# Making the next slice's token operands from set 3 on, with another sum and high-part tile, and one buffer each for the gated rows and P1's copy

## The chip, the cores and the metric

The kernel runs on one core of a Trainium2 chip. The metric is the time of the whole program on the device, in microseconds (us). Of the core's engines five matter here: TensorE (PE; matrix products, with the weight loads shown as PEld), VectorE (DVE), ScalarE (ACT), GpSimd (POOL) and SyncE (SP), of which the last two mostly issue DMAs in this program. TensorE writes its results into PSUM, 8 banks of 128 x 512 numbers; the operands lie in SBUF; large intermediates go to DRAM and come back by DMA.

## What is computed

A linear attention is followed by two layers, both of them chains of matrix products, on 3072 tokens. The first layer has a product of two gates, the second a Gelu (the sigmoid form). The change is in the second layer's first product, `x @ w_in`, with the Gelu behind it:

```
for t in range(S):
    state = gamma[None, :, None, None] * state + np.einsum('bhd,bhe->bhde', k[:, :, t], v[:, :, t])
    y[:, :, t] = scale * np.einsum('bhd,bhde->bhe', q[:, :, t], state)
...
a = x @ w1
b = x @ w2
h = a * b @ w3
return (h @ w_out).astype(np.float32)
...
h = x @ w_in                                # 3072 x 512 by 512 x 2048
g = h * (1.0 / (1.0 + np.exp(-1.702 * h)))
return (g @ w_out).astype(np.float32)       # 3072 x 2048 by 2048 x 512
```

All is float32. A product keeps that precision by three matmuls: each operand is split into a high part (`fp32r`) and a low part, what is left of it, and high x high, high x low and low x high are added up in one bank (`mm3`, L256 to L259).

## The kernel before

The program runs in stages: attention with the first gates, the gates (`psm`), the first layer's second half (`blend`, tiles `h`, `wh`), then `Expand` (`x @ w_in` and the Gelu), then `contract` (`g @ w_out`). The change is in `Expand`, in `operands`, which makes its token operands, and in a table of the last stage's opening work.

`Expand` uses a scheme of seven products P1 to P7 in place of eight (Strassen's, in Winograd's form): two blocks of 512 tokens and two halves of the 512 dimensions on one side, a 2 x 2 grid of weight blocks on the other. **A slice** is a pair of token blocks; there are three. **A set** is one call of `quad` (L643): all seven products for one group of 256 of the 2048 columns. A slice has eight sets, numbered 0 to 7 here, so there are 24. One product is 6 matmuls (two 128-row steps, three matmuls each), one set 42.

In a set TensorE makes P1 (bank `a`), P5 (bank `e`), then P4 of the set before (into that set's bank `a`), P6 (added onto P1), P2 (bank `c`), P7 (added onto the same `a`), P3 (added onto P5). ScalarE copies the sums out between them, `s1` after P1, `s5` after P5, `u2` after P6, `u3` after P7 (`copy`, L607), so P6 can't start ahead of the end of the copy `s1`, nor P7 ahead of `u2`. VectorE adds P2 to `s1` (L659), `s5` to `u3` (L662) and P3 to `u2` (L665). The Gelus of a set run in the next set (`fourth`, L619): `g[:, 0]` from `s1`, `b12` from `u2`, then P4, `g[:, 2]` from `u3` and `g[:, 1]` from the bank. The three gated rows in `g` are stored to DRAM (L628), VectorE makes four sums of them into `t` (L636), and `t` is stored too (L637). `s1` and `g` have two buffers, taken in turn (`s0`/`s1`, `g0`/`g1`); `t` has one.

**The token operands** of a slice are seven pairs of high and low tiles, 128 x 1024 each: four quarters of the token blocks (P1: b11, P2: b21, P3: b22, P7 or the like: their sums). `operands` (L516) is a generator that is advanced one step at a time: loads, then sums (`sub`, VectorE), then splits: a cast to the high tile (ScalarE in slices 1 and 2, VectorE for slice 0) and a subtraction on VectorE for the low one. `quad` calls `step(0)` to `step(3)` at four places of a set, behind P4 (0), P6 with the Gelus and sums of the set before (1), P7 (2) and P3 (3). A pair (set, step) in the table `NEXT` advances the next slice's generator there; the loads are at (2, 3), and some steps are left to the first set of the slice that reads the operands (L691). For slice 0 the generator is advanced in the turns of `blend` (`ahead`). The tiles' homes are handed on from product to product by `Homes`: an operand takes the home of one that the old slice has read for the last time.

**The weights** are split likewise by `split_left` in ScalarE and VectorE, seven times in the first sets (`SPLIT`); in slice 0 sets 0 to 5 do one each, in slices 1 and 2 one set each. `OPENING` lists what the last slice does ahead of `contract`: loads of its first operands, splits of them in eight pieces (`opening_split`, VectorE), and the split of its first weight in two halves (`split_w`, L744 and L745, on VectorE).

Each engine runs its instructions in the order in which the code issues them. Stores and loads above are issued on SP's queue; the contraction's first weight is loaded from POOL's.

Of the kernel before, what the change touches and what calls it, by code (L numbers as in the profile page):

```python
# [7 lines left out]
F32 = mybir.dt.float32  # L8
# [37 lines left out]
def tile_kernel(  # L46
# [469 lines left out]
    def operands(s, copy, pool):  # L516
# [26 lines left out]
        yield  # L543
        t, t7 = (pool.tile([P, 2, TB], F32, tag=f"yt{n}", name="yt") for n in range(2))
        sub(t, b12, b11)
        yield
        sub(t7, b22, b12)
        yield
        split("P1", b11, raws[0])
        yield  # L550
        give("P1", "P5")
        split("P5", t, ys_homes.tile("l"))
        sub(t, b22, t)
        yield
        split("P6", t, ys_homes.tile("l"))
        sub(t, b21, t)
        give("P6")
        yield
        give("P2", "P7", "P3", "P4")
        split("P2", b21, raws[3])  # L560
        split("P7", t7, raws[1])
        yield
        split("P3", b22, raws[2])
        yield
        split("P4", t, ys_homes.tile("l"))
        yield
# [26 lines left out]
    class Expand:  # L593
# [25 lines left out]
        def fourth(self):  # L619
            a, s, j, n, s1, u2, u3 = self.open  # L620
            g, b12 = self.value(f"g{n % 2}", 3), self.value("b")
            self.gated(g[:, 0], s1)
            self.gated(b12, u2)
            self.product(a, "P4", s, j)
# [18 lines left out]
        def quad(self, s, j, n, step):  # L643
            a, e, c = (self.bank(x) for x in "aec")
            self.product(a, "P1", s, j, True)
            s1 = self.copy(a, f"s{n % 2}")
            self.product(e, "P5", s, j, True)
            s5 = self.copy(e, "s5")
            fourth = self.fourth() if self.open else iter((0, 0))
            next(fourth)  # L650
# [18 lines left out]
        def run(self):  # L669
# [3 lines left out]
            for n in range(1, NQ - 1):  # L673
                fetch_left(n, nc.sync)
            for tag in ("s1", "s5", "u2", "u3", "s0", "b"):
                self.value(tag)
            for tag, m in (("t", 4), ("g0", 3), ("g1", 3)):
                self.value(tag, m)
            ys_homes.add(self.p, l=3, h=1)
            split_left(1, nc.vector.tensor_copy)  # L680
            for s, order in enumerate(QUADS):
                for at_j, j in enumerate(order):

                    def step(at):
                        nonlocal nxt
                        at = at_j, at
                        more = s + 1 < NS
                        if more and at == (2, 3):
                            nxt = operands(s + 1, nc.scalar.copy, self.py)
                            next(nxt)  # L690
                        elif (more and at in NEXT) or (s and at in ((0, 0), (0, 1), (0, 2))):  # L691
                            next(nxt)
                        if not more:
                            for run in OPENING.get(at, ()):
                                run()

                    self.quad(s, j, s * NQ + at_j, step)
# [5 lines left out]
    SPLIT = {j: j + 2 for j in range(NQ - 2)} | {NQ + 4: 0, 2 * NQ + 2: 7}  # L703
    NEXT = (4, 3), (5, 3), (6, 0), (7, 0), (7, 1)
    RIGHT = dict(P1=0, P2=1, P3=2, P5=3, P6=4, P7=5, P4=6)
# [58 lines left out]
    for n in range(2):  # L764
        OPENING[7, 1 + 2 * n] = [
            lambda n=n: split_w("P1", 5, n * KH, n * KH + KH, nc.vector.tensor_copy)
        ]
    for k, at in enumerate(
        ((4, 1), (4, 2), (4, 3), (5, 0), (5, 1), (5, 3), (6, 1), (6, 3))
    ):  # L770
# [184 lines left out]
    with tc.manual_schedule():  # L955
# [180 lines left out]
        def ahead(n):  # L1136
# [7 lines left out]
            elif early is None:  # L1144
# [3 lines left out]
                )  # L1148
                ys_homes.add(py, l=8, h=7)
                early = operands(0, nc.vector.tensor_copy, py)  # L1150
# [127 lines left out]
```

## Time and profile before

| | us |
|---|---|
| median of three runs | 979.91 |
| the runs | 979.59, 979.91, 981.85 |
| the profiled execution, whole | 981.67 |
| its span, first to last instruction | 979.8 |
| TensorE busy in it | 950.6 (97%) |
| VectorE, ScalarE, GpSimd busy | 706.9 (72%), 430.7 (44%), 227.7 (23%) |
| `Expand`, from its first P1 to the contraction's first matmul | 505.0 to 745.6 |

How to read the rows below. Times are from the start of the span. A row of the timeline gives start and length in us, the engine, the line, the operation, what it writes and reads, the shape and, in brackets, how long the engine stood idle before it and what released it. In the list of waits a row gives who waited for whom, the total in us, how often and the longest. A row of the groups by line gives the busy time in us and the mean length in ns, then idle time before it. A row of the DMA issues gives the number, the size and the us from issue to landing. A row of the windows gives the stretch, each engine's busy time, the granted clock of TensorE as a share of 2.4 GHz, the share of DMA time and GB/s. Names leave out buffer numbers, so `s` is `s0`, `s1` or `s5`, and `g` is `g0` or `g1`.

### The profile page before, as it was taken

The page shows a single profiled execution, that of the slowest core. Times are in us where ns is not written, and L with a number is a line of the kernel's source. Part 1 is how long each engine was busy: PE and PEld are TensorE (multiplying, and loading weights), DVE is VectorE, ACT ScalarE, POOL GpSimd, SP SyncE. Part 2 cuts the span into 40 slices and gives each one's busy share as a digit, 9 for nine tenths or more (in the row PEclk, how much of TensorE's full clock was granted, in tenths as well). Part 3 has the DMA queues.
Part 4 walks back from the last instruction along what each step waited for, and adds up shares of the span by engine and source line. Part 5 has one row for each costly group of instructions (what it writes and reads, how often), then busy time and mean ns, then how long its engine had stood idle before and what let it go on. Part 6 is the DMA issues. An engine that isn't in the chain of part 4 may idle for free.

```text
span 979.8 us, 14573 instructions
## 1 busy us (share of the span) xinstructions
PE 950.6 (97%) x5656; PEld 782.1 (80%) x5656; DVE 706.9 (72%) x857; ACT 430.7 (44%) x643; POOL 227.7 (23%) x281
## 2 busy tenths in 40 slices
PE   5899999999999999999999999998999999999998
PEld 5777877888888888888888877886887888888886
DVE  6898878989889876856975766566577575467652
ACT  4555444432322212744536665554544544354430
POOL 6422000479677884511020000000000000000000
PEclk9999999999999999999999999999999999999999
DMA  9999765679998999899786634843986967766861
GB/s 351 400 351 347 277 205 198 210 248 351 323 369 294 349 344 400 283 344 316 245 304 227 271 156 191 308 177 127 327 306 249 343 236 270 249 213 235 288 228 54
DMA packets 87188, 268.50 MB, mean 274 GB/s; under 512 B 7152, under 2 KB 15600, under 8 KB 79056
## 3 DMA queue, kind: packets, MB, share of 16 engines
q1 hardware_dynamic: 71136, 188.60, 53.9%
q0 software_dynamic: 15840, 78.91, 21.1%
q8 instruction: 44, 0.72, 0.3%
q14 instruction: 24, 0.20, 0.1%
q10 hardware_dynamic: 144, 0.07, 0.0%
HBM read 166.37 MB, written 101.19 MB: 273 GB/s over the span
## 4 chain that ended last, share of the span: by engine, by line
PE 86%; DVE 6%; DMA 4%; ACT 2%; issue 1%; POOL 0%; DVEq 0%; POOLq 0%; ACTq 0%; SPq 0%
PE m L259 12%; PE m L258 12%; PE m L257 12%; PE psm L257 7%; PE psm L258 7%; PE psm L259 7%; PE a L257 4%; PE a L258 4%; PE a L259 4%; DMA qkv<-in_qkv_dram 2%; PE e L258 2%; PE e L259 2%; PE e L257 2%; PE psg L257 2%; PE y L440 1%; DMA raw<-in_w_dram 1%
## 5 line engine op out<-in xcount | busy, mean ns | idle before, releaser
L257 PE MATMUL psm<-xh,wh 128*128 128x512 f32 x320 | 124.5, 389 | 0.0
L258 PE MATMUL psm<-xl,wh 128*128 128x512 f32 x320 | 124.5, 389 | 0.0
L259 PE MATMUL psm<-xh,wl 128*128 128x512 f32 x320 | 124.5, 389 | 0.0
L257 PE MATMUL m<-h,op 128*128 128x512 f32 x320 | 124.5, 389 | 0.0
L259 PE MATMUL m<-h,op 128*128 128x512 f32 x320 | 124.5, 389 | 0.0
L258 PE MATMUL m<-l,op 128*128 128x512 f32 x304 | 118.3, 389 | 0.0
L732 ACT CAST h<-l 128x2048 fp32r<-128x2048 f32 x38 | 72.3, 1914 | 82.5 <-PE m L259 63.6
L733 DVE TENSOR_TENSOR l<-l,h 128x2048 fp32r<-128x2048 f32 x38 | 85.4, 2286 | 17.0 <-ACT h L732 16.9
L738 POOL DMA_DIRECT2D op<-sw x6 | 3.2, 532 | 401.9 <-PE a L259 223.1
L139 ACT ACTIVATE x<-raw 128x512 f32<-128x512 f32 x72 | 46.8, 674 | 71.1 <-DMA raw<-in_wo_dram 38.1
L257 PE MATMUL a<-yh,op 128*128 128x512 f32 x192 | 75.2, 392 | 0.0
L258 PE MATMUL a<-yl,op 128*128 128x512 f32 x192 | 75.0, 391 | 0.0
L259 PE MATMUL a<-yh,op 128*128 128x512 f32 x192 | 74.9, 390 | 0.0
L257 PEld LDWEIGHTS m<-h,op 128*128 128x128 f32 x320 | 60.1, 188 | 12.6
L259 PEld LDWEIGHTS psm<-xh,wl 128*128 128x128 f32 x320 | 60.1, 188 | 12.6
L257 PEld LDWEIGHTS psm<-xh,wh 128*128 128x128 f32 x320 | 60.1, 188 | 12.5
L259 PEld LDWEIGHTS m<-h,op 128*128 128x128 f32 x320 | 60.1, 188 | 12.5
L258 PEld LDWEIGHTS psm<-xl,wh 128*128 128x128 f32 x320 | 60.1, 188 | 12.3
L258 PEld LDWEIGHTS m<-l,op 128*128 128x128 f32 x304 | 57.1, 188 | 11.8
L257 PE MATMUL m<-h,wh 128*128 128x512 f32 x168 | 65.4, 389 | 0.0
L259 PE MATMUL m<-h,wl 128*128 128x512 f32 x168 | 65.4, 389 | 0.0
L173 DVE TENSOR_TENSOR l<-l,h 128x2048 fp32r<-128x2048 f32 x19 | 43.5, 2291 | 21.7 <-ACT h L272 20.2
(172 smaller groups left out, 2102.0 us busy)
## 6 DMA issues: line engine op xcount, KB each, us to landing
l<-gd SPq DMA_DIRECT2D x38, 1024.0 KB, 6.4
gd<-t SPq DMA_DIRECT2D x24, 1024.0 KB, 4.9
qkv<-in_qkv_dram POOLq DMA_DIRECT2D x20, 1024.0 KB, 8.8
l<-hd SPq DMA_DIRECT2D x19, 1024.0 KB, 8.0
gd<-g SPq DMA_DIRECT2D x24, 768.0 KB, 3.3
raw<-in_w_dram SPq DMA_DIRECT2D x30, 512.0 KB, 5.6
hd<-g POOLq DMA_DIRECT2D x12, 1280.0 KB, 7.4
raw<-in_wo_dram SPq DMA_DIRECT2D x24, 512.0 KB, 6.9
```

What stands on the lines that cost most here:

```text
L139: nc.scalar.activation(x, high, AF.Abs, scale=2.0**16)
L173: nc.vector.tensor_tensor(lo, x, hi.bitcast(F32), ALU.subtract)
L257: nc.tensor.matmul(ps, wh, xh, start=start, stop=False, skip_group_check=True)
L258: nc.tensor.matmul(ps, wh, xl, start=False, stop=False, skip_group_check=True)
L259: nc.tensor.matmul(ps, wl, xh, start=False, stop=stop, skip_group_check=True)
L440: nc.tensor.matmul(out_y, vs[c][:, 2 * p + j, :], pt[c][:, j, p, :], start=(c % NCK == 0 and p < 2), stop=True, skip_group_check=True,)
L732: nc.scalar.copy(hi, x.bitcast(F32))
L733: nc.vector.tensor_tensor(x, x.bitcast(F32), hi.bitcast(F32), ALU.subtract)
L738: queue.dma_start(t.bitcast(F32), sw[PART[name]])
```

## The change

Three things are changed.

1. In `operands` there are three tiles for sums in place of two, and the order of steps is another: t, t6, t4 (the sums for P5, P6, P4), then the splits of P1, P2, P5 with the sum for P7, P6, P7, P3, P4. `NEXT` has eight places in place of five, from (3, 3) on, and two steps (P3, P4) are left to the first set of the slice that reads them, in place of three (P2 with P7, P3, P4). The pool `y` has a low home less; the pool of `Expand` has one low and one high home more.
2. `g` and `s1` have one buffer each. So that the next copy can go into `s1`, the first Gelu of the set before is issued ahead of the copy of P1 in place of behind that of P5 (`next(fourth)` stands there once more).
3. In the last slice `split_w` moves from (7, 1) and (7, 3) to (7, 0) and (7, 1), and four of the eight `opening_split` pieces to earlier places.

```diff
-        t, t7 = (pool.tile([P, 2, TB], F32, tag=f"yt{n}", name="yt") for n in range(2))
+        t, t6, t4 = (
+            pool.tile([P, 2, TB], F32, tag=f"yt{n}", name="yt") for n in range(3)
+        )
         sub(t, b12, b11)
         yield
-        sub(t7, b22, b12)
+        sub(t6, b22, t)
+        yield
+        sub(t4, b21, t6)
         yield
         split("P1", b11, raws[0])
         yield
+        split("P2", b21, raws[3])
+        yield
         give("P1", "P5")
         split("P5", t, ys_homes.tile("l"))
-        sub(t, b22, t)
+        sub(t, b22, b12)
         yield
-        split("P6", t, ys_homes.tile("l"))
-        sub(t, b21, t)
         give("P6")
+        split("P6", t6, ys_homes.tile("l"))
         yield
+        split("P7", t, raws[1])
         give("P2", "P7", "P3", "P4")
-        split("P2", b21, raws[3])
-        split("P7", t7, raws[1])
         yield
         split("P3", b22, raws[2])
         yield
-        split("P4", t, ys_homes.tile("l"))
+        split("P4", t4, ys_homes.tile("l"))
         yield
...
-            g, b12 = self.value(f"g{n % 2}", 3), self.value("b")
+            g, b12 = self.value("g", 3), self.value("b")
             self.gated(g[:, 0], s1)
+            yield
             self.gated(b12, u2)
             self.product(a, "P4", s, j)
             yield
...
+            fourth = self.fourth() if self.open else iter((0, 0, 0))
             self.product(a, "P1", s, j, True)
-            s1 = self.copy(a, f"s{n % 2}")
+            next(fourth)
+            s1 = self.copy(a, "s1")
             self.product(e, "P5", s, j, True)
             s5 = self.copy(e, "s5")
-            fourth = self.fourth() if self.open else iter((0, 0))
             next(fourth)
...
-            ys_homes.add(self.p, l=3, h=1)
+            ys_homes.add(self.p, l=4, h=2)
...
-                        elif (more and at in NEXT) or (s and at in ((0, 0), (0, 1), (0, 2))):
+                        elif (more and at in NEXT) or (s and at in ((0, 0), (0, 1))):
...
-    NEXT = (4, 3), (5, 3), (6, 0), (7, 0), (7, 1)
+    NEXT = (3, 3), (4, 3), (5, 1), (5, 3), (6, 2), (7, 0), (7, 1), (7, 3)
...
-        OPENING[7, 1 + 2 * n] = [
+        OPENING[7, n] = [
...
-        ((4, 1), (4, 2), (4, 3), (5, 0), (5, 1), (5, 3), (6, 1), (6, 3))
+        ((4, 1), (4, 2), (4, 3), (5, 0), (5, 1), (5, 2), (5, 3), (6, 0))
...
-                ys_homes.add(py, l=8, h=7)
+                ys_homes.add(py, l=7, h=7)
```

Three places show how instructions stand before and after. The numbers in names tell buffers of one tag apart, and the words in brackets the semaphores that an instruction waits for (DMAHW is a DMA from SP's queue).

ScalarE in set 4 of slice 0, before (`s0` is the copy of P1 of this set, `s1` that of set 3):

```order
L607 COPY u3_5121<-a_5060 128x512 [waits PE_49,Activation_49]
L607 COPY s0_5140<-a_5131 128x512 [waits PE_49]
L607 COPY s5_5148<-e_5132 128x512 [waits DVE_49,PE_49]
L617 ACTIVATE g1_5150<-s1_5069 128x512 [waits DMAHW1_49]
L617 ACTIVATE b_5151<-u2_5095 128x512 [waits DVE_49]
L607 COPY u2_5166<-a_5131 128x512 [waits PE_49,Activation_49]
L617 ACTIVATE g1_5150<-u3_5121 128x512
```

and in the change:

```order
L611 COPY u3_5120<-a_5059 128x512 [waits PE_49,Activation_49]
L621 ACTIVATE g_5143<-s1_5071 128x512 [waits DMAHW7_49,DVE_49,Activation_49]
L611 COPY s1_5146<-a_5134 128x512 [waits PE_49,Activation_49]
L611 COPY s5_5154<-e_5135 128x512 [waits DVE_49,PE_49]
L621 ACTIVATE b_5144<-u2_5094 128x512 [waits DVE_49]
L611 COPY u2_5169<-a_5134 128x512 [waits PE_49,Activation_49]
L621 ACTIVATE g_5143<-u3_5120 128x512
```

The Gelu of `s1` into `g` now stands ahead of the copy of P1 and waits for a DMA, VectorE and ScalarE itself; before, it stood behind the copy of P5 and waited for a DMA only, that of the store two sets back.

VectorE from step (7, 1) of slice 0 to P2's sum in set 0 of slice 1, before (`yl` are low parts: of P6, then P2 and P7, then P3):

```order
L530 TENSOR_TENSOR yl_5400<-yt_5202,yh_5401 128x1024
L534 TENSOR_TENSOR yt_5202<-yl_5055,yt_5202 128x1024
L659 TENSOR_TENSOR s1_5358<-c_5351,s1_5358 128x512
L662 TENSOR_TENSOR u3_5418<-u3_5418,s5_5366 128x512
L665 TENSOR_TENSOR u2_5389<-e_5350,u2_5389 128x512
L530 TENSOR_TENSOR yl_5055<-yl_5055,yh_5457 128x1024
L530 TENSOR_TENSOR yl_5053<-yt_5203,yh_5460 128x1024
L636 TENSOR_TENSOR t_5474<-b_5448,g1_5447 128x512
L636 TENSOR_TENSOR t_5474<-g1_5447,b_5448 128x512
L636 TENSOR_TENSOR t_5474<-g1_5447,t_5474 128x512 x2
L530 TENSOR_TENSOR yl_5054<-yl_5054,yh_5480 128x1024
L659 TENSOR_TENSOR s0_5437<-c_5430,s0_5437 128x512
```

and in the change (`yl` of P6, then P7 and P3, then P4):

```order
L530 TENSOR_TENSOR yl_5404<-yt_5131,yh_5405 128x1024
L665 TENSOR_TENSOR s1_5365<-c_5355,s1_5365 128x512
L668 TENSOR_TENSOR u3_5421<-u3_5421,s5_5373 128x512
L671 TENSOR_TENSOR u2_5393<-e_5354,u2_5393 128x512
L530 TENSOR_TENSOR yl_5052<-yt_5130,yh_5431 128x1024
L530 TENSOR_TENSOR yl_5053<-yl_5053,yh_5463 128x1024
L641 TENSOR_TENSOR t_5477<-b_5444,g_5443 128x512
L641 TENSOR_TENSOR t_5477<-g_5443,b_5444 128x512
L641 TENSOR_TENSOR t_5477<-g_5443,t_5477 128x512 x2
L530 TENSOR_TENSOR yl_5483<-yt_5132,yh_5484 128x1024
L665 TENSOR_TENSOR s1_5446<-c_5436,s1_5446 128x512
```

The sum behind P6's low part is gone from here (t4 is made in set 5), P2's low part too, and P7's and P3's come one place earlier.

VectorE in the last set of slice 2, from u2's sum of the set before to its own, with the casts and subtractions of the first contraction weight (L744 and L745, then L750 and L751), before:

```order
L665 TENSOR_TENSOR u2_6510<-e_6476,u2_6510 128x512
L758 CAST op_6446<-op_6295 128x512
L759 TENSOR_TENSOR op_6295<-op_6295,op_6446 128x512
L636 TENSOR_TENSOR t_6590<-b_6570,g0_6569 128x512
L636 TENSOR_TENSOR t_6590<-g0_6569,b_6570 128x512
L636 TENSOR_TENSOR t_6590<-g0_6569,t_6590 128x512 x2
L744 CAST op_6596<-op_6521 128x1024
L745 TENSOR_TENSOR op_6521<-op_6521,op_6596 128x1024
L659 TENSOR_TENSOR s1_6559<-c_6552,s1_6559 128x512
L662 TENSOR_TENSOR u3_6612<-u3_6612,s5_6567 128x512
L665 TENSOR_TENSOR u2_6585<-e_6551,u2_6585 128x512
L744 CAST op_6596<-op_6521 128x1024
```

and in the change:

```order
L671 TENSOR_TENSOR u2_6515<-e_6479,u2_6515 128x512
L750 CAST op_6580<-op_6526 128x1024
L751 TENSOR_TENSOR op_6526<-op_6526,op_6580 128x1024
L641 TENSOR_TENSOR t_6594<-b_6561,g_6560 128x512
L641 TENSOR_TENSOR t_6594<-g_6560,b_6561 128x512
L641 TENSOR_TENSOR t_6594<-g_6560,t_6594 128x512 x2
L750 CAST op_6580<-op_6526 128x1024
L751 TENSOR_TENSOR op_6526<-op_6526,op_6580 128x1024
L665 TENSOR_TENSOR s1_6563<-c_6553,s1_6563 128x512
L668 TENSOR_TENSOR u3_6615<-u3_6615,s5_6571 128x512
```

The first half's split went ahead of the four sums, the second half's ahead of the add into `s1`; the last pieces of `opening_split` (L758 and L759) left this place.

## Rows read from the trace of the kernel before

**Rows 1.** The page, busy time of TensorE.

```profile
PE 950.6 (97%) x5656; PEld 782.1 (80%) x5656; DVE 706.9 (72%) x857; ACT 430.7 (44%) x643; POOL 227.7 (23%) x281
```

**Rows 2.** List of TensorE's waits, whole span: total, times, longest.

```profile
PE s L374 <- DMA qkv<-in_qkv_dram: 11.0, 6, 4.7
PE e L258 <- DVE yl L530: 3.7, 2, 1.9
PE c L257 <- ACT yh L529: 3.6, 2, 1.8
PE c L258 <- DVE yl L530: 1.5, 2, 0.8
PE m L259 <- DVE op L745: 1.1, 2, 0.5
```

**Rows 3.** Timeline of ScalarE: P1's copies around both changes of slice.

```profile
571.84 0.59 ACT L607 COPY s<-a 128x512 f32<-128x512 f32 x1 [2.08 <-PE a L259]
581.36 0.59 ACT L607 COPY s<-a 128x512 f32<-128x512 f32 x1 [1.50 <-PE a L259]
596.16 0.59 ACT L607 COPY s<-a 128x512 f32<-128x512 f32 x1 [3.28 <-PE a L259]
...
662.80 0.59 ACT L607 COPY s<-a 128x512 f32<-128x512 f32 x1 [1.50 <-PE a L259]
679.18 0.59 ACT L607 COPY s<-a 128x512 f32<-128x512 f32 x1 [4.88 <-PE a L259]
```

**Rows 4.** Windows after the second change of slice (clock third from the end).

```profile
675.10:678.80 3.70, 3.70 (x11) 2.89 (x10) 2.59 (x4) 0.00 (x0) 0.00 (x0) 0.54 0.48 195
```

**Rows 5.** Timeline of TensorE where the contraction starts.

```profile
745.62 0.47 PE L257 MATMUL m<-op 128*128 128x512 f32 x1
...
751.09 0.39 PE L258 MATMUL m<-op 128*128 128x512 f32 x1
```

**Rows 6.** Groups by line, shapes apart: casts and subtractions for the operands.

```profile
L529 ACT CAST yh<-yt 128x1024 fp32r<-128x1024 f32 x8 | 8.4, 1046 | 1.5 <-DVE yt L534 1.5
...
L530 DVE TENSOR_TENSOR yl<-yt,yh 128x1024 fp32r<-128x1024 f32 x12 | 14.7, 1222 | 8.0 <-ACT yh L529 7.8
L534 DVE TENSOR_TENSOR yt<-yl 128x1024 f32<-128x1024 f32 x6 | 7.3, 1217 | 0.0
```

**Rows 7.** Timeline of VectorE, last set: first half of the contraction weight.

```profile
744.86 0.69 DVE L744 CAST op<-op 128x1024 fp32r<-128x1024 f32 x1
745.58 1.22 DVE L745 TENSOR_TENSOR op<-op 128x1024 fp32r<-128x1024 f32 x1
```

**Rows 8.** Timeline of set 4 of slice 0: VectorE, ScalarE, TensorE.

```profile
543.06 0.68 DVE L659 TENSOR_TENSOR s<-c,s 128x512 f32<-128x512 f32 x1
...
543.28 0.59 ACT L607 COPY s<-a 128x512 f32<-128x512 f32 x1 [1.71 <-PE a L259]
...
545.12 0.63 ACT L617 ACTIVATE g<-s 128x512 f32<-128x512 f32 x1
...
545.80 0.39 PE L257 MATMUL a<-yh,op 128*128 128x512 f32 x1
```

**Rows 9.** Timeline of VectorE, set 0 of slice 1: the add into s1.

```profile
583.20 0.68 DVE L659 TENSOR_TENSOR s<-c,s 128x512 f32<-128x512 f32 x1
```

**Rows 10.** Line L628, the store of g: least, median and most.

```profile
DMA to landing us min/median/max: 3.2/3.3/7.2
```

**Rows 11.** Timeline of SyncE: the three latest-landing stores of g in Expand's sets.

```profile
539.52 0.32 SPq L628 DMA_DIRECT2D gd<-g  x1
...
620.96 0.32 SPq L628 DMA_DIRECT2D gd<-g  x1
...
732.55 0.32 SPq L628 DMA_DIRECT2D gd<-g  x1
```

**Rows 12.** DMA issues in windows around 539.5, 621.0, 732.6 and 723.1.

```profile
gd<-g SPq DMA_DIRECT2D x1, 768.0 KB, 6.3
...
gd<-g SPq DMA_DIRECT2D x1, 768.0 KB, 5.2
...
gd<-g SPq DMA_DIRECT2D x1, 768.0 KB, 7.2
...
gd<-g SPq DMA_DIRECT2D x1, 768.0 KB, 4.8
```

More of the change, by code (lines that the diff above doesn't have):

```diff
@@ L674, in run @@
                 fetch_left(n, nc.sync)
-            for tag in ("s1", "s5", "u2", "u3", "s0", "b"):
+            for tag in ("s5", "u2", "s1", "u3", "b"):
                 self.value(tag)
-            for tag, m in (("t", 4), ("g0", 3), ("g1", 3)):
+            for tag, m in (("t", 4), ("g", 3)):
                 self.value(tag, m)
-            ys_homes.add(self.p, l=3, h=1)
+            ys_homes.add(self.p, l=4, h=2)
             split_left(1, nc.vector.tensor_copy)
```

## The prediction

> **What bounds the kernel now.** The page first: TensorE is busy 950.6 of 979.8 us [rows 1], so a change can only win where TensorE stands still. The list of its waits names all such places [rows 2]: the loads at the start, which this change doesn't touch, and four rows that belong to the stage changed here. Three of them (the banks e and c, 3.7 + 3.6 + 1.5 us, twice each) are the first set of slices 1 and 2, where P2 and P3 wait for their token operands; the fourth (m, 1.1 us) is the start of the contraction.
>
> These rows hold the idle time alone, and a pipelined matmul hides part of a stall in its own length. So I price each place from end to end. ScalarE copies product P1 of every set, right when it is done; the distance from one such copy to the next is a set's time [rows 3]. Undisturbed it is 581.36 - 571.84 = 9.52 us, that is 42 matmuls of 0.2267. At the first change of slice it is 596.16 - 581.36 = 14.80, at the second 679.18 - 662.80 = 16.38: **5.28 and 6.86 us too much**. The second is longer by 1.58 because the granted clock stood at 0.54 (nearly all of it at the lower level, 1.2 GHz) from 675.1 to 678.8, just after two stalls [rows 4]. At the contraction's start there are 16 steps from the matmul at 745.62 to that at 751.09: 5.47 - 16 x 0.2267 = **1.84 us** too much [rows 5].
>
> **What the change removes.** Each split of an operand is a cast on ScalarE of 1.05 us and a subtraction on VectorE of 1.22; the sums cost 1.22 each [rows 6]. Seven splits and four sums per slice stay; none is added or dropped. Before, P2's and P7's casts and subtractions stood in the first set of the slice that reads them. Now P1 is split at the end of set 5 of the slice ahead, P2 in set 6 and P7 at the end of set 7; only P3 and P4 stay behind. The casts of P1 and P2 stand on ScalarE behind u3's copy (P7 is done at 8.4 of a set's 9.5 us), so they end 0.4 to 0.8 us into the next set, before its P1 is done at 1.6: nothing. No DMA changes its place on SP's or POOL's queue. P3 is read last in its set: its cast takes the place that P2's had (after the second Gelu), VectorE has by then only P7's subtraction ahead of it, and its first matmul comes six products after the set began, 8.2 us by rows 3. Cast and subtraction in turn (1.05 + 1.22) from about 4.4 us on, when the Gelus are through, end near 6.7. Cover left: 1.5 us. So I take both swaps as gone: -5.28 - 6.86, the low clock included, since the stalls ahead of it go.
>
> The halves of the first contraction weight were split on VectorE in the last set after its four sums, and behind u2's add [rows 5, 7]; now both come one step of the set earlier or more. The first half's cast waits for the load and for P4 of the set before, whose weight lies in its home: third product of the last set, done some 4.3 us into it (three products of 9.52 / 7 and 0.2 for the drain, an estimate). Cast and subtraction, 0.69 + 1.22, end near 6.2; the contraction starts behind the eighth product, at 10.9. The second half takes the place that the first had, ending at 745.58 + 1.22 = 746.80, and its first matmul is 12 steps after 745.62, at 748.3. I take -1.84. Gain in all: 5.28 + 6.86 + 1.84 = 13.98 us.
>
> **What it adds.** Two buffers become one, and the first Gelu of the set before now stands ahead of P1's copy on ScalarE. It waits (a) for VectorE's add into s1, (b) for the landing of the last store of the gated rows from the one buffer g. Behind it on ScalarE's queue stands the copy of P1, then that of P5; for P1's copy TensorE waits before P6, which adds into the same bank.
>
> How much room is there? In set 4 P1's copy began at 543.28 and P6's first matmul at 545.80, 2.52 us later [rows 8]. Gelu and copy take 0.63 + 0.59 = 1.22. So whatever releases the Gelu later than 545.80 - 1.22 = 544.58, 1.30 us after P1 is done, stops TensorE.
>
> (a) The add into s1 of set 3, behind a weight's subtraction on VectorE, ended at 543.06 + 0.68 = 543.74 [rows 8]: 0.84 us to spare. In set 5 of slice 0 the new sum for P4 (1.22) stands ahead of that add on VectorE, and the weight's subtraction too: 0.38 us late, so 0.4. In slice 1 no weight is split there, so nothing. At the swap the add ended at 583.20 + 0.68 = 583.88 [rows 9]; one sum (1.22) leaves the queue ahead of it, so 582.66, and with the Gelu no longer between P5's copy and the cast of P5's operand (0.5) some 582.1. The limit is 581.36 + 1.30 = 582.66: cost between 0 and, if only one of the two holds a little less, 0.5 each. I take 0.
>
> (b) A store lands 3.3 us after its issue at the median, 3.2 at least [rows 10]. In set 3 it was issued at 539.52 [rows 11], so the limit 544.58 allows 5.06 us. Of the 22 stores that a later set's P1 copy has to wait for, 19 keep that. Three don't [rows 12], in the order of rows 11: 6.3 us behind the four token loads in slice 0 (545.82, 1.24 us late), 5.2 behind those in slice 1 (626.16; P1's copy there is at 596.16 + 3 x 9.52 = 624.72, limit 626.02, 0.14 late), and 7.2 beside the contraction weight's load in the last set (739.75; copy at 679.18 + 6 x 9.52 = 736.30, limit 737.60, 2.15 late). The fourth row of 12, 4.8, keeps it by 0.3. All these transfers are issued where they were, relative to TensorE, so I expect the same landings. With 0.1 each for the restart (an idle TensorE's first matmul in rows 5 is 0.47 long, the others 0.39): 1.3 + 0.2 + 2.3 = 3.8. Bounds: 0, if the stores should land early, and about 6, if each is a further 0.7 late.
>
> The weight's load comes from POOL's queue and the store from SP's, and the store beside it is still the slowest. The Trainium skill (DMA: Bandwidth & Descriptors, Issuing engines are not separate DMA queues) says that DMAs of all issuing engines run on the same 16 engines and interleave. The row agrees; if queues did not interfere, the 2.3 would be 0 and the sum 969.5.
>
> At the end of the blend, slice 0's operands now take two more turns. P3 and P4 (a VectorE cast and a subtraction each, about 1.9 us) come just ahead of the first set, P4 then 13 us ahead of its use; the weight split behind them is due a set later. I cost it at nothing.
>
> **Sum.** The profiled execution took 981.67 us (span 979.8 and 1.9 around it): 981.67 - 13.98 + 0.4 + 3.8 = 971.9. The median of the runs is 979.91, 1.8 below the profiled one, about what the low clock cost; I take it that the median had none of it: 979.91 - (13.98 - 1.58) + 4.2 = 971.7. Forecast **971.8 us**, 0.8% less.
>
> **Rivals.**
> 1. *The store's wait costs nothing.* If the three late landings don't come back, only 0 to 0.4 is paid: 979.91 - 12.40 + 0.2 = 967.7. For it: no DMA time repeats exactly (6.3 and 5.2 for the same pattern). Against: the bytes ahead of them are the same. Chance 0.12.
> 2. *More stalls than three sets.* A landing later by 0.7 in those sets and in the 4.8 one, 0.5 at each swap, a stretch at the lower clock after the 2.3 us stall (1.6): 3 x 0.7 + 0.5 + 2 x 0.5 + 1.6 = 5.2, so up to 977.0. Chance 0.14.
> 3. *Faster in the swaps, lost in every set.* One buffer instead of two exposes the store each time. The loss eats the gain of 12.4 when each of 22 sets stalls 0.56, that is from landings of 5.06 + 0.56 = 5.6 us; with 6.3 in every set it is 22 x 1.3 = 28.6, so 996. Against: the median of 3.3 [rows 10]. Near 5.6 the time is the same (0.05), beyond it slower (0.07). The Trainium skill (Trainium Kernel Development and Optimization, Best Practices) asks to double-buffer so that DMA overlaps compute, which speaks against this edit; the trace agrees in three sets of 22 only, since the reader comes back so late that one buffer covers the store.
>
> **Chances and range.** Forecast 0.62 (970 to 973.5); rivals as above. Within 0.3% (977.0 to 982.9) two measurements can't be told apart. Faster 0.88, same 0.05, slower 0.07. The range leaves out rival 3 and the ends of rivals 1 and 2: 967.5 to 976.5.
>
> **What would show it.** After the change the list of TensorE's waits should have no row for operands yl or yh and none for the contraction weight. In their place there should be waits of the P6 matmul (bank a) on ScalarE's copy into s1, in set 4 of slice 0 (about 1.3 us) and in the last set (about 2.2), small ones in set 6 of slice 0 and set 4 of slice 1; ScalarE's first Gelu should name the store of g as what released it there. Wrong would be: a wait on yl or yh that stays (then a cover was miscounted), the Gelu waiting for the store in most sets (rival 3), or a gain with none of these waits (rival 1).

## The result: 0.9% less time, and five short waits in place of the long ones

The changed kernel takes **971.03 us** (median of five runs, 969.88 to 974.57); the kernel before took 981.15 beside it (979.59 to 981.96). The ratio is 0.9906, with a 95% interval of 0.9884 to 0.9927. The profiled execution took 971.65, with a span of 969.9. The forecast was 971.8, between 967.5 and 976.5.

The page of the changed kernel, part 1 (busy us, share of the span, instructions); TensorE was busy for 950.6 of 979.8 before [rows 1]:

```profile
PE 948.6 (98%) x5656; PEld 781.6 (81%) x5656; DVE 706.9 (73%) x857; ACT 431.7 (45%) x643; POOL 226.4 (23%) x281
```

TensorE's waits from 500 us on, changed kernel (who waited for whom, us in total, times, longest). The four rows of [rows 2] that belonged to this stretch have gone, and one row has come:

```profile
PE a L257 <- ACT s L611: 1.7, 3, 1.2
```

That is P6, which waits for ScalarE's copy of P1. The list holds idle time only. From start to start of the matmuls there are five places, all at the first matmul of P6 (each with some 0.11 for that matmul, which takes 0.34 instead of 0.23): 1.52 us in set 4 of slice 0, 0.59 in set 6 of slice 0, 0.10 at the first set of slice 2, 0.30 in set 4 of slice 1 and 0.43 in the last set. Together 2.94, where the kernel before lost 13.8 by the same reading.

Timeline of the largest, set 4 of slice 0 (start, length; in brackets idle time and what ended it):

```profile
546.46 0.39 PE L259 MATMUL a<-yh,op 128*128 128x512 f32 x1
546.79 0.63 ACT L621 ACTIVATE g<-s 128x512 f32<-128x512 f32 x1 [4.33 <-DMA gd<-g]
547.46 0.59 ACT L611 COPY s<-a 128x512 f32<-128x512 f32 x1
548.09 0.50 PE L257 MATMUL a<-yh,op 128*128 128x512 f32 x1 [1.24 <-ACT s L611]
```

ScalarE stands idle for 4.33 us until the store of g lands, then come the Gelu and the copy, and then P6. The first row shows that TensorE had started its previous matmul 1.63 earlier. The last set has the same chain, much shorter:

```profile
729.29 0.63 ACT L621 ACTIVATE g<-s 128x512 f32<-128x512 f32 x1 [3.62 <-DMA gd<-g]
...
730.59 0.50 PE L257 MATMUL a<-yh,op 128*128 128x512 f32 x1 [0.16 <-ACT s L611]
```

The stores behind these waits, in the DMA issues of the windows around 540.5, 619 and 722 (KB, us from issue to landing); they answer to [rows 12]:

```profile
gd<-g SPq DMA_DIRECT2D x1, 768.0 KB, 6.3
...
gd<-g SPq DMA_DIRECT2D x1, 768.0 KB, 5.1
...
op<-sw POOLq DMA_DIRECT2D x1, 1024.0 KB, 6.1
gd<-g SPq DMA_DIRECT2D x1, 768.0 KB, 5.2
```

Set 6 of slice 0 has another cause. VectorE, ScalarE and TensorE there:

```profile
562.63 2.03 DVE L173 TENSOR_TENSOR op<-op 128x1792 fp32r<-128x1792 f32 x1
...
564.57 1.22 DVE L534 TENSOR_TENSOR yt<-yl,yt 128x1024 f32<-128x1024 f32 x1
565.71 0.69 DVE L665 TENSOR_TENSOR s<-c,s 128x512 f32<-128x512 f32 x1
...
566.48 0.63 ACT L621 ACTIVATE g<-s 128x512 f32<-128x512 f32 x1 [2.44 <-DVE s L665]
...
567.14 0.59 ACT L611 COPY s<-a 128x512 f32<-128x512 f32 x1
...
567.78 0.50 PE L257 MATMUL a<-yh,op 128*128 128x512 f32 x1 [0.31 <-ACT s L611]
```

A weight's subtraction and the new sum for P4 (L534) stand ahead of the add into s1; the Gelu waits for that add, the copy for the Gelu, P6 for the copy.

What was to be covered is covered. P3's low part in the first set of slice 1, and the second half of the contraction weight with the contraction's first matmul:

```profile
588.55 1.23 DVE L530 TENSOR_TENSOR yl<-yl,yh 128x1024 fp32r<-128x1024 f32 x1 [0.99 <-ACT yh L529]
...
591.30 0.39 PE L258 MATMUL e<-yl,op 128*128 128x512 f32 x1
...
736.22 1.23 DVE L751 TENSOR_TENSOR op<-op 128x1024 fp32r<-128x1024 f32 x1
...
737.55 0.39 PE L257 MATMUL m<-op 128*128 128x512 f32 x1
```

P3's subtraction ends at 589.78 and is first read at 591.30: 1.52 us of cover. The weight's second half ends at 737.45, and is read 12 steps after 737.55.

### The profile page after: what moved, and what is told of

Read it like the earlier page. It is cut to its first block, busy times and chain, and to the rows that moved or that the text cites. A ratio compares the mean times of both kernels' runs of the same rounds, so it can differ in the third digit from the quotient of the medians.

```text
span 969.9 us, 14620 instructions
## 1 busy us (share of the span) xinstructions
PE 948.6 (98%) x5656; PEld 781.6 (81%) x5656; DVE 706.9 (73%) x857; ACT 431.7 (45%) x643; POOL 226.4 (23%) x281
## 4 chain that ended last, share of the span: by engine, by line
PE 89%; DMA 5%; DVE 3%; ACT 2%; issue 1%; POOL 0%; SPq 0%; ACTq 0%; DVEq 0%; POOLq 0%
PE m L258 12%; PE m L257 12%; PE m L259 12%; PE psm L257 7%; PE psm L258 7%; PE psm L259 7%; PE a L257 4%; PE a L259 4%; PE a L258 4%; DMA qkv<-in_qkv_dram 2%; PE e L258 2%; PE e L259 2%; PE e L257 2%; PE psg L257 2%; PE psw L259 1%; PE psg L259 1%
## 5 line engine op out<-in xcount | busy, mean ns | idle before, releaser
L257 PE MATMUL psm<-xh,wh 128*128 128x512 f32 x320 | 124.5, 389 | 0.0
L257 PE MATMUL m<-h,op 128*128 128x512 f32 x320 | 124.5, 389 | 0.0
L744 POOL DMA_DIRECT2D op<-sw x6 | 3.2, 533 | 391.0 <-PE a L259 213.6
L257 PE MATMUL a<-yh,op 128*128 128x512 f32 x192 | 75.3, 392 | 1.7 <-ACT s L611 1.7
L257 PEld LDWEIGHTS m<-h,op 128*128 128x128 f32 x320 | 60.1, 188 | 12.6
L257 PEld LDWEIGHTS psm<-xh,wh 128*128 128x128 f32 x320 | 60.1, 188 | 12.5
L258 PEld LDWEIGHTS m<-l,op 128*128 128x128 f32 x304 | 57.1, 188 | 11.8
L257 PE MATMUL m<-h,wh 128*128 128x512 f32 x168 | 65.4, 389 | 0.0
```

The source lines that it names most:

```text
L257: nc.tensor.matmul(ps, wh, xh, start=start, stop=False, skip_group_check=True)
L258: nc.tensor.matmul(ps, wh, xl, start=False, stop=False, skip_group_check=True)
L744: queue.dma_start(t.bitcast(F32), sw[PART[name]])
```

## The experiments

Two readings serve all of them: the median beside the kernel before on the same chip, and, since the time up to the first copy of P1 varies by 3 us from trace to trace (505.8 to 508.9, with no regard to the kernel), the stretch of the profiled execution from that copy to the end.

| kernel | median, us | kernel before beside it | first P1 copy | span | from that copy on |
|---|---|---|---|---|---|
| before (profile of [rows 1 to 12]) | | 981.15 | 506.6 | 979.8 | 473.2 |
| changed | 971.03 | 981.15 | 507.4 | 969.9 | 462.4 |
| after_again | 970.63 | 980.72 | 505.8 | 967.8 | 461.9 |
| sum_later | 969.70 | 980.72 | 506.6 | 967.3 | 460.7 |
| loads_apart | 971.39 | 980.72 | 507.8 | 971.9 | 464.1 |
| pair | 968.42 | 980.72 | 506.2 | 966.6 | 460.4 |
| opening_only | 979.15 | 979.73 | 506.2 | 976.1 | 469.9 |
| buffers_only | 982.30 | 979.73 | 505.8 | 978.9 | 473.1 |
| weight_sp | 970.68 | 979.73 | 506.8 | 968.3 | 461.5 |
| **pair_moved** | **967.97** | 979.73 | 507.2 | 966.5 | 459.3 |
| twice | 992.27 | 980.12 | 505.8 | 989.8 | 484.0 |
| pair_twice | 988.13 | 980.12 | 508.9 | 986.7 | 477.9 |
| weight_sp_first | 970.88 | 980.12 | 506.9 | 968.3 | 461.4 |

The theory to test: P6 waits for the copy of P1, the copy for the Gelu that now stands ahead of it, and the Gelu for one of two things, the store of g where it lands late, or the add into s1 where VectorE is late. The rivals: the waits come from the single buffers in every set, or from the moved operands, or would only move elsewhere.

**The changed kernel again.**

> The changed kernel once more, on the chip of the three runs beside it. All theories: 969.5 to 971.7. The theory (P6 waits for P1's copy, and that copy for the Gelu ahead of it, which waits for the store of g or for the add into s1) expects the same five waits on bank a as in its first profile, 2.9 us in all: 1.5 in set 4 of slice 0, 0.6 in set 6 of slice 0, 0.3 in set 4 of slice 1, 0.1 at the second change of slice, 0.4 in the last set. Open is the last set: if a landing is fixed by what is issued ahead of it, the store of g lands there after 5.2 us again; if it hangs on the execution, it can be 5 to 7 and the wait 0.4 to 2.3.

Measured: 970.63. Four of the five waits come back within 0.02 us (1.53, 0.58, 0.32, 0.10), the stores behind the token loads landing after 6.3 and 5.1. The fifth doesn't: the store of g in the last set landed after 4.5, and there is no wait. So the landings behind the token loads come back (in three later traces the first of them is 5.7 to 5.8); the one beside the contraction weight does not.

**The new sum one step later.**

```
-    NEXT = (3, 3), (4, 3), (5, 1), (5, 3), (6, 2), ...
+    NEXT = (3, 3), (4, 3), (5, 2), (5, 3), (6, 2), ...
```

> The changed kernel, with the new sum for P4 one step later in set 5, behind VectorE's adds into s1 and u3 instead of ahead of them. Theory: the 0.6 us that TensorE loses in set 6 of slice 0 go, nothing else changes: 971.0 - 0.6 = 970.4; the add into s1 of set 5 in slice 0 begins some 1.2 us sooner. Rival (the subtraction for the weight ahead of it, 2.03 us, is enough to hold the add): the wait stays, 971.0.

Set 5 of slice 0 in this kernel:

```profile
563.19 0.68 DVE L665 TENSOR_TENSOR s<-c,s 128x512 f32<-128x512 f32 x1
...
564.39 1.22 DVE L534 TENSOR_TENSOR yt<-yl,yt 128x1024 f32<-128x1024 f32 x1
```

The add stands ahead of the sum now, and set 6 has no wait. 969.70, 0.9 below after_again's 970.63. The ranges overlap (969.07 to 973.09 against 969.54 to 970.85), so the median alone wouldn't show 0.6; the missing wait does.

**Token loads two by two.**

```
+            if n == 2 and s:
+                yield
             nc.sync.dma_start(b, yd[2 * s + h][:, 2 * k : 2 * k + 2])
...
-    NEXT = (3, 3), (4, 3), ...
+    NEXT = (3, 3), (4, 2), (4, 3), ...
```

> The changed kernel, with the next slice's four token loads issued two by two, in sets 2 and 3, instead of all four in set 2. Theory (the store of g lands late in set 3 since those loads are under way): with half of them ahead the store lands some 3.3 to 4.9 us after its issue, under the 5.06 that are allowed, in set 3 and in set 4 alike; the waits of 1.5 us in slice 0 and 0.3 in slice 1 go: 971.0 - 1.8 = 969.2. Rival (something else makes that store late, such as the stores themselves): landing 6.3 and 5.1 as before, 971.0. Second rival (the lateness is shared out over two sets): two waits of 0.2 to 0.5 per slice, 970 to 971.

The stores of g around 540.5, 617.5 and 722 here:

```profile
gd<-g SPq DMA_DIRECT2D x1, 768.0 KB, 4.2
...
gd<-g SPq DMA_DIRECT2D x1, 768.0 KB, 3.3
...
op<-sw POOLq DMA_DIRECT2D x1, 1024.0 KB, 8.3
gd<-g SPq DMA_DIRECT2D x1, 768.0 KB, 7.4
```

The first two fall from 6.3 and 5.1, and their waits are gone: the token loads were the cause. (The sum for P5 moves by a step as well; the landings are read directly.) Yet the time does not fall, because in this execution the third store landed after 7.4. That cost more than the two others together. Timeline of the last set:

```profile
728.29 0.39 PE L259 MATMUL a<-yh,op 128*128 128x512 f32 x1
729.75 0.63 ACT L625 ACTIVATE g<-s 128x512 f32<-128x512 f32 x1 [5.83 <-DMA gd<-g]
...
731.04 0.50 PE L257 MATMUL a<-yh,op 128*128 128x512 f32 x1 [2.37 <-ACT s L615]
```

The window behind it (each engine's busy time; the granted clock is third from the end):

```profile
731.00:736.00 5.00, 4.96 (x15) 3.91 (x16) 2.11 (x4) 2.61 (x5) 0.00 (x0) 0.66 0.06 23
```

TensorE stands still for 2.37 us, and soon after the granted clock is 0.66 for five us, a part of them at the lower level, 1.2 GHz. The stall costs 2.6 and the clock 1.6. The runs of this kernel spread from 967.94 to 974.49; of these two there is no trace, but the slowest shows the mean clock of the profiled execution, 0.996, and the fastest 1.000. This is the last-set wait that the forecast had put at 2.3.

**P1's copy first again, without a further buffer.**

```
-            next(fourth)
-            s1 = self.copy(a, "s1")
+            s1 = self.copy(a, f"s{n % 2}")
             self.product(e, "P5", s, j, True)
-            s5 = self.copy(e, "s5")
+            next(fourth)
+            s5 = self.copy(e, f"s{1 - n % 2}")
...
```

> The changed kernel, with P1's copy first again and the first Gelu behind it. That needs no further buffer: the copies of P1 and P5 share two buffers and change places from set to set, so that P1 is copied into the buffer that P5 had (free since the set before) and P5 into the one that the Gelu has just read. Theory: P6 is no longer held by the Gelu; only u2's copy is, which has 4.08 + 0.57 - 1.79 = 2.86 us from P1's end to the Gelu's start instead of 1.30. The latest Gelu so far was 1.4 us beyond the old limit, so all five waits go: 971.0 - 2.9 = 968.1, and no row for a<-s in the list of TensorE's waits. Rival (the waits only move, to P7 on u2's copy or to VectorE's sums): 970 to 971, with new rows for u.

Set 4 of slice 0 on ScalarE:

```profile
544.05 0.59 ACT L611 COPY s<-a 128x512 f32<-128x512 f32 x1 [2.87 <-DVE u L668]
...
545.47 0.63 ACT L621 ACTIVATE g<-s 128x512 f32<-128x512 f32 x1 [0.83 <-DMA gd<-g]
```

The store that the Gelu waits for, in the DMA issues around 539, and then TensorE's waits from 500 us on:

```profile
gd<-g SPq DMA_DIRECT2D x1, 768.0 KB, 6.2
```

```profile
PE a L257 <- ACT s L611: 0.2, 1, 0.2
```

The store lands as late as before, and the Gelu waits for it as before, but P1 has been copied by then and TensorE doesn't stand still. 968.42, as expected (968.1). Something was left: P1's copy now waits for VectorE's add into u3 (line 668 in the first row), and in set 6 of slice 0 that is behind the new sum. With the changes of slice it makes 0.98 us.

**The same, with those adds freed.** Two entries of the table move and the weight's load goes to SP's queue:

```
-    NEXT = (3, 3), (4, 3), (5, 1), (5, 3), (6, 2), (7, 0), (7, 1), (7, 3)
+    NEXT = (3, 3), (4, 3), (5, 2), (5, 3), (6, 2), (7, 0), (7, 2), (7, 3)
...
-    OPENING[6, 1] = [lambda: load_w("P1", 4)]
+    OPENING[6, 1] = [lambda: load_w("P1", 4, nc.sync)]
```

> The kernel called pair (P1's copy first, the copies of P1 and P5 sharing two buffers) lost 0.98 us in Expand: 0.5 in set 6 of slice 0, where P1's copy waits for VectorE's add into u3 behind the new sum for P4 and a weight's subtraction, 0.1 and 0.35 at the changes of slice, where the add into u3 stands behind the subtraction of P6's operand. Here the sum goes one step later in set 5 and P6's split one step later in set 7, each behind the adds, and the contraction weight is loaded from SP's queue. Theory: all three waits go, nothing else changes: 968.4 - 0.9 = 967.5, and no row for Expand in the list of TensorE's waits. Rival (P6's operand, now split a step later, comes late, or the adds are held by something else): 968 to 969, with a row for yh, yl or s.

The window 520 to 745 of the changed kernel, then of this one (TensorE's busy time comes first):

```profile
520.00:745.00 225.00, 223.25 (x980) 183.30 (x979) 157.87 (x216) 129.77 (x209) 0.54 (x1) 1.00 0.65 248
```

```profile
520.00:745.00 225.00, 225.00 (x994) 186.16 (x993) 158.04 (x216) 129.08 (x209) 0.00 (x0) 1.00 0.65 250
```

TensorE is busy for the whole window, and the list of its waits has no row from 500 us on. The stretch from the first P1 copy is 459.3, that is 13.9 below the kernel before: the whole gain of 13.98 that the forecast had worked out ahead of any cost. Median 967.97, ratio to the kernel before 0.9879 (0.9860 to 0.9897). That is 3 us below the changed kernel by the medians. From pair (ratio 0.9876, 0.9860 to 0.9893) the times can't tell it apart, so the last 0.98 us show in the traces alone.

**One part alone: the contraction weight's split.** The change's lines for `OPENING`, in the kernel before.

> The kernel before, with the third part of the change alone: both halves of the first contraction weight and the last token pieces are split where the changed kernel splits them. Theory: the 1.84 us that TensorE loses at the contraction's start go, and both changes of slice stay: 1.8 below the kernel before on the same chip (980.7 would become 978.9), no row for the contraction's weight in the list of TensorE's waits, the rows for yl and yh as in [rows 2]. Rival (the late store and load of the last set hold the weight, so that the wait stays): 980.7.

```profile
PE c L257 <- ACT yh L529: 3.6, 2, 1.8
PE e L258 <- DVE yl L530: 2.1, 2, 1.9
PE c L258 <- DVE yl L530: 1.5, 2, 0.8
```

In the list of waits from 500 us on, the row for the weight (m) is gone; the other rows of [rows 2] stay. So the cause is shown, but not its size: 0.6 less by the medians, ratio 0.9993 (0.9981 to 1.0006), where 1.8 would be 0.9982, just inside; the next experiment shows that 1.8 is a size of one execution. In the trace the stretch is even 3.3 shorter. Of that 1.8 is the contraction's start; the rest comes from this execution's low clock, which fell into the first change of slice, ahead of P3, and took up part of P3's wait (the row e of the list, 2.1 instead of 3.7). So it cost nothing: both changes of slice are 14.84 us from copy to copy here, where the kernel before had 14.80 and 16.38. The window there, granted clock 0.62:

```profile
588.00:592.50 4.50, 4.36 (x12) 3.23 (x12) 4.39 (x7) 2.22 (x4) 0.00 (x0) 0.62 0.43 175
```

**One part alone: the single buffers.** The change's lines for `fourth`, `quad` and the tags, in the kernel before.

> The kernel before, with the second part of the change alone: one buffer for g, one for P1's copy, the first Gelu ahead of that copy; the token operands stay as they were. Theory: slower than before by the stores that land late, 1.5 us in set 4 of slice 0, 0.3 in set 4 of slice 1, 0.4 to 2.6 in the last set by the landing of that execution, and no wait in set 6 of slice 0, since the new sum is not there: 980.7 + 2.2 to 4.4 = 982.9 to 985.1. Rival (one buffer costs in every set): 22 rows or more on bank a. Second rival (it costs nothing, the changed kernel's five waits come from the moved operands): 980.7.

```profile
PE e L258 <- DVE yl L530: 3.7, 2, 1.9
PE a L257 <- ACT s L607: 2.8, 3, 1.3
PE c L258 <- DVE yl L530: 1.5, 2, 0.8
PE c L257 <- ACT yh L529: 0.6, 2, 0.3
PE m L259 <- DVE op L747: 0.3, 1, 0.3
```

Slower by the medians, 982.30 against 979.73, ratio 1.0026 (1.0013 to 1.0039). Waits on bank a stand in set 4 of slice 0 (1.6) and of slice 1 (0.4), not in every set, and none in set 6 of slice 0, as the theory has it. What it hadn't foreseen: at each change of slice P6 now waits first, 1.0 from start to start, and P2 (c, L257) 1.5 less, so that the change of slice itself costs 0.5 less.

In the profiled execution the last store landed after 4.1, with no wait. The contraction's start (m) lost 0.57 from start to start, where the kernel before lost 1.8, though VectorE's order there is the same. The first of the four sums tells why, in the kernel before and here:

```profile
742.25 0.69 DVE L636 TENSOR_TENSOR t<-b,g 128x512 f32<-128x512 f32 x1 [4.17 <-DMA gd<-t]
...
739.62 0.69 DVE L637 TENSOR_TENSOR t<-b,g 128x512 f32<-128x512 f32 x1 [1.15 <-DMA gd<-t]
```

The sum waits for the store of the t before it. That landed after 8.0 us in the kernel before, and after 5.0 here and 5.2 in opening_only. So the next sum began at 742.85 in the kernel before, 1.3 after the end of the Gelu of u3 that it reads (741.55), and here right behind that Gelu; the weight's split stands behind these sums. So some 1.2 of the 1.84 belong to the late transfers of that one execution. With this and the changes of slice the stretch here comes out as long as the kernel before's. Why the median is 2.6 longer isn't settled by this trace: its waits on bank a and the changes of slice make 1.0.

The first part of the change was not run alone. That the changes of slice go by it follows from the last two runs, where the rows for yl and yh stay, and from pair_moved, which has it.

**The weight's load from SP's queue.** First in its step (6, 1), then in (6, 0):

```
-    OPENING[6, 1] = [lambda: load_w("P1", 4)]
+    OPENING[6, 0] = [lambda: load_w("P1", 4, nc.sync)]
```

> The changed kernel, with the first contraction weight loaded from SP's queue instead of POOL's; its step and its bytes stay. So far that load took 5.0, 5.2, 5.4, 6.1, 8.0 and 8.3 us in six executions, and the store of g issued 2.8 us behind it landed 0.9 sooner after its issue than that each time (4.1 to 7.4). Theory 1 (the load on POOL's queue is what varies): from SP it takes about as long as the other loads of its size, 5 to 6, the store lands under 5.06, the last set has no wait; median 970.5, and the executions spread less than the 969.5 to 974.5 seen so far. Theory 2 (the DMA engines vary there whatever the queue): the same spread, landings up to 7.

> The changed kernel with the first contraction weight loaded from SP's queue, this time issued ahead of the store of g, as POOL issues it (in weight_sp it came behind that store and so said nothing of the queue). In eight executions with POOL's load the store of g landed after 7.2, 5.2, 4.5, 4.1, 4.3, 7.4, 4.4 and 4.1 us. Theory 1 (the scatter is POOL's queue): load 5 to 5.5, store 4.1 to 4.5, no wait in the last set in any execution, none of the times above 971.5. Theory 2 (the load beside it is the cause whatever its queue): landings of 4.1 to 7.4 here too and single times up to 974.

The DMA issues around the load, first of weight_sp, then of weight_sp_first:

```profile
op<-sw SPq DMA_DIRECT2D x1, 1024.0 KB, 7.1
gd<-g SPq DMA_DIRECT2D x1, 768.0 KB, 3.3
```

```profile
op<-sw SPq DMA_DIRECT2D x1, 1024.0 KB, 6.2
gd<-g SPq DMA_DIRECT2D x1, 768.0 KB, 5.1
```

In step (6, 1) SP issues the load behind the stores of its set, so the first run didn't test the queue; it shows that the store lands after 3.3 once no load is ahead of it, and the last set has no wait (970.68, expected 970.5). The second run has the order of the changed kernel, and both durations lie among POOL's (5.0 to 8.3 and 4.1 to 7.4). One time of five is above 971.5 (972.64). That speaks against theory 1. How wide the scatter from SP's queue is, one trace can't tell.

**Every g stored twice.** A second store, to a place that nothing reads, goes behind the first in `fourth`:

```
...
             nc.sync.dma_start(gd[s][:, j, :3], g)
+            nc.sync.dma_start(gx[s][:, j], g)
```

> The changed kernel with every g stored twice, the second time to a place that nothing reads, so that the one buffer comes free later in every set (768 KB more are written per set). This goes for the turning point of the third rival: a landing of 5.06 us after the issue is allowed, and each set stalls by what is beyond it. Estimate of the second landing: 768 KB land in 3.25, the 1024 KB of t in 4.1, so 1536 KB in some 5.8 after the first issue. Theory: 0.8 us in each of 19 sets and about 3 in the three late ones: 971 + 15 + 7 = 993, with 20 or more rows of waits on bank a behind P1's copy, and the Gelu released by the store. Rival (the second store hardly lengthens the first one's landing, or the add into s1 is the later release): 971 to 975.

> The kernel called pair (P1's copy first, P1's and P5's copies sharing two buffers) with the same second store of g. In pair the Gelu may start 2.86 us after P1 is done instead of 1.30, so a landing of 5.06 + 1.56 = 6.6 is allowed. Theory: some 5.8 in the usual set stay hidden and only the three or four late stores stall, by about 1.5 to 2 each: 968.4 + 6 = 974, some 19 us less than the changed kernel with two stores. Rival (it is not the Gelu's place that counts but the store's landing as such, or the landing of t, which comes 1.7 later too): 985 or more.

The two stores of a usual set of twice (DMA issues around 576), and its waits of TensorE in Expand:

```profile
gd<-g SPq DMA_DIRECT2D x1, 768.0 KB, 3.3
gx<-g SPq DMA_DIRECT2D x1, 768.0 KB, 4.8
```

```profile
PE a L258 <- ACT s L612: 14.6, 14, 4.4
```

The same waits of pair_twice, and its stores behind the token loads (DMA issues around 542):

```profile
PE a L258 <- ACT u L612: 8.4, 3, 3.6
PE a L258 <- ACT s L612: 2.7, 4, 1.8
```

```profile
gd<-g SPq DMA_DIRECT2D x1, 768.0 KB, 8.1
gx<-g SPq DMA_DIRECT2D x1, 768.0 KB, 9.5
```

Twice: 992.27 where 993 was expected, but by other parts. In a usual set the second landing comes 0.4 + 4.8 = 5.2 after the first issue, not 5.8, and costs 0.4, not 0.8; the set behind the token loads costs 4.9 in slice 0, and 2.2 more by a stretch at the lower clock. Still, the third rival is real: push the landing past the limit, and nearly every set pays.

Pair_twice was forecast wrong: 988.13, not 974. In the usual sets the waits do go, as the theory says; of the nine places over 0.2 us that are left, most stand at the changes of slice and where the loads are. But behind the token loads the second store lands after 9.5 (and 9.9 in slice 1), which the forecast had put near 6.6 + 2. Three waits of P7 on u2's copy, one there in each of the two slices and one in the last set, make 8.4 us, the longest 3.6, and in two places the granted clock falls. More room ahead of a wait helps while the lateness is smaller than the room.

## Why the prediction was right, step by step

| term | forecast | in the profiled execution | in other traces |
|---|---|---|---|
| two changes of slice, low clock included | -5.28 - 6.86 | gone, but for 0.10 | gone |
| contraction's start | -1.84 | gone | gone; the kernel before's order loses 0.57 in buffers_only |
| sum ahead of the add into s1 | +0.4 | +0.59 | 0.57 to 0.58; none in sum_later and pair_moved |
| store in set 4 of slice 0 | +1.3 | +1.52 | 0.92 to 1.53; none in loads_apart |
| store in set 4 of slice 1 | +0.2 | +0.30 | 0.23 to 0.42; none in loads_apart |
| store in the last set | +2.3 | +0.43 | none to 4.2, the low clock behind it included |

**The removed part** was right in its places, and against the execution that it was read from also in its size. The best proof is pair_moved, which keeps the change's operands and takes away the waits it added: 13.9 of 13.98. But two of its sizes are that execution's own: 1.84 at the contraction's start, of which 1.2 came from a late store of t, and the 1.58 of the low clock, which cost nothing in opening_only.

**The chain that the change adds** was named rightly, with its sets: bank a, three stores of 22, and one add. Its room was taken as 1.30 us and is 1.12. The reader finds the 0.18 in the first timeline above: the Gelu starts 0.10 after the landing (540.41 + 6.28 = 546.69, then 546.79), the copy 0.67 behind it where 0.63 was counted, P6 0.63 behind the copy where 0.59 was counted. So a landing may take 4.87 us, not 5.06. With that, 6.28 gives 1.41 and 5.06 gives 0.19, to which the slow first matmul adds 0.11: 1.52 and 0.30, as measured.

**The last set's term** was mis-sized. The step that failed is "I expect the same landings", taken from one execution. In the two sets behind the token loads it holds (6.2 to 6.4, and 5.7 to 5.8 in three traces; 5.0 to 5.2). In the last set the landing was 7.2 in the trace of before, and 5.2, 4.5, 4.1, 4.3, 7.4, 4.4 and 4.1 in later ones with the load from POOL ahead of it: by the limit of 4.87, six of these eight cost 0.4 or nothing in the changed kernel's order. The two others would cost 2.4 and 2.6; the 7.4 did, in loads_apart, and brought the low clock. The usual landing would have made the term about zero.

**The starting point** was off in two ways. The forecast took the median of the kernel before as free of the low clock and cut the gain by 1.58; but the 11 runs of it beside after_again all show a mean granted clock of 0.993 to 0.997. And the median of five runs is 981.15, not 979.91. With the terms of these traces it reads 981.15 - 13.98 + 2.94 = 970.1; measured is 971.03, 0.9 more. It is the same with pair_moved, 11.8 below the kernel before by the medians and 13.9 by the traces. A part of the difference is in the two sizes above: without the 1.2 and the 1.58 the gain is 11.2 instead of 13.98. How often executions of the kernel before have the one or the other stays open, since there is one trace of it.

So the forecast came within 0.8 with errors that stood against each other: 1.9 in the last set on the one side, 0.6 in the other waits and 1.2 in the base on the other; whether the 1.58 was rightly taken off, the traces don't settle. That the number came so near is in part luck. The places and the chain of waits were not.

**The rivals.** The first (the store costs nothing) is what pair and pair_moved made true, at 968.4 and 968.0 against its 967.7. The second shows in single executions: 973.69 in the trace of loads_apart, and perhaps 974.49 there and 974.57 of the changed kernel, of which there is no trace. The third needed a second store in every set to come true.

## What to carry to other kernels

A wait is priced by what stands behind the waiting instruction on its engine: one buffer for g is enough as long as nothing that TensorE needs soon stands behind the Gelu that waits for it, and where two buffers that exist changed places (pair_moved), no wait was left that another buffer could have taken away. Take a time for a step from several executions before it becomes a term, above all for DMA transfers that run beside others; here the same late transfers made one term of the cost too large and one of the gain. Fill the gaps in an engine's queue behind the adds that others wait for, not ahead of them.

## What the runs showed of the hardware

- The same load, with the same transfers ahead of it at the same distances, took 5.0, 5.0, 5.2, 5.3, 5.4, 6.1, 8.0 and 8.3 us in eight executions. The store issued 2.8 us behind it, from another queue, landed 1.9 us after the load in each of them (1.86 to 1.92), and 1.87 after it in weight_sp_first, where both come from SP's queue. So the store's lateness is the load's. The Trainium skill (DMA: Bandwidth & Descriptors, Queues, rings and completion order) says that a semaphore increment lands only after every earlier write of that DMA engine, across its queues; these rows agree. They would look the same if the store's bytes were only moved in turn behind the load's: in twice the second of two stores of 768 KB lands 1.9 us after the first, with no such load ahead of them.
- What lengthens the load was not found. In the trace of the kernel before, the DMA moved 436 GB/s from 737 to 738 us, and 31, 25 and 16 in the three microseconds from 739 on, until the late stores of g and t had landed.
- TensorE's granted clock fell to its lower level after a wait of 2.4 us in the last set of loads_apart, and behind the two stalls at a change of slice ([rows 4]); behind the waits of up to 1.2 us in the changed kernel it stayed at 1.00. The same stalls didn't bring it each time: it fell at the second change of slice only in the kernel before, and at the first only in opening_only and buffers_only.
- The first matmul behind such a wait takes 0.34 us from start to start, the others 0.23.
